# Four groups of scale columns in place of five in the K projection of a DiT block

## The chip, the cores and the metric

The kernel runs on one core of one Trainium2 chip. The metric is the device time of one execution in microseconds (us); the number for a kernel is the median of its runs. A core has five engines with queues of their own: TensorE (PE; its weight loads are listed as PEld), VectorE (DVE), ScalarE (ACT), GpSimd (POOL) and SyncE (SP), which here issues nearly all of the transfers from memory. Engines wait for each other, and for transfers, by semaphores.

## The reference

One block of a diffusion transformer on two batches of 256 tokens, width D = 1152, two heads:

```python
B, N, D = (2, 256, 1152)          # F = 4 * D
mod = (_silu(c) @ w_mod).reshape(B, 6, 1, D)
shift_a, scale_a, gate_a, shift_m, scale_m, gate_m = [mod[:, i] for i in range(6)]
h = _layernorm(x, axis=-1) * (1 + scale_a) + shift_a
qkv = (h @ wqkv).reshape(B, N, 3, H, Dh)
...
x = x + gate_a * a
h2 = _layernorm(x, axis=-1) * (1 + scale_m) + shift_m
m = _gelu(h2 @ w_fc1) @ w_fc2
return x + gate_m * m
```

The part that matters here is `h`, without its shift, and the K third of `h @ wqkv`.

## The kernel before

The 512 tokens are four tiles of 128 (tiles 0 and 1 are batch 0, tiles 2 and 3 batch 1). The width of 1152 is nine chunks of 128. The kernel runs through its stages in one written order; at its end a loop (L813 to L823) ties every instruction to the one before it on its engine, so each engine's order is that of the program text.

**Loads.** SP issues, in this order, the four tiles of x (L86) and then, by the list `SGROUPS` (L98), for each group of chunks the columns of the scale part of `w_mod` that belong to it (`w_scale_a`, L107) and the rows of `w_k` that belong to it, without their last three column blocks (`load_k`, L104). The first group's rows go as two transfers, one for each row, the others' as one. Then come the last three column blocks of all rows of `w_k` (L113), the shift columns (L129), `w_q` (L134) and the rest. A load of columns a-b of the scale moves 128 partitions x 9 rows x (b - a + 1) x 128 values of two bytes, so a group of one, two or three chunks is made of pieces of 256, 512 or 768 bytes.

**Front.** ScalarE and VectorE make the layer norm's statistics; `norm1` writes the normalized tokens `xn`; TensorE transposes them chunk by chunk (`transpose_x`, L264) into PSUM tiles `pt`. The factor 1 + scale_a of a chunk comes from `scale_group` (L241): nine products of 128x128 weights with two columns for each chunk, written to a PSUM tile `pm`; `scale_add` (L253) adds 1 to it on VectorE and stores it in `scale_a`. `pm` and `pt` share two PSUM buffers in turn ("aux"). `both` (L317) then scales a transposed chunk into `hT0`: batch 0 on VectorE (L270), after it batch 1 on ScalarE (L272). A chunk is then ready for `k_step(k)`, whose matmuls (L280) add chunk k's part of the K projection to six PSUM tiles, `pk[0]` to `pk[5]`.

**The loop around the change** (L396 to L404) does this for steps k = 3 to 8:

```python
    for k in range(3, KD):
        split = 2 if k == 5 else 0
        k_step(k, 0, T, 0, split)
        if k in (3, 5, 7):
            k1 = min(k + 3, KD)
            scale_add(scale_group(k + 1, k1), k + 1, k1)
        if k < KD - 1:
            both(transpose_x([k + 1], range(NT)), k + 1)
        k_step(k, 0, T, split)
```

So ahead of step 3's six matmuls come the scale products of chunks 4-5 (18 of them) and chunk 4's four transposes; ahead of step 4's, chunk 5's transposes; inside step 5, after two of its matmuls, the products of chunks 6-7 and chunk 6's transposes; ahead of step 6's, chunk 7's transposes; ahead of step 7's, the products of chunk 8 and its transposes. Chunks 0 to 3 are served by the code above the loop (L360 to L395), which the diff leaves alone. After the loop, `k_evac` (L405) empties the six tiles and `k_panel` (L437) computes the last three column blocks of K. The Q projection (L521), attention (L556, L639), V (L599), the output projection (L690) and the MLP (L743, L799) follow.

Of the kernel before, what the change touches and what calls it, by code (L numbers as in the profile page):

```python
# [19 lines left out]
def kernel(  # L20
# [20 lines left out]
    KD = D // P  # L41
# [18 lines left out]
    def acc_tile(shape, name, dt=FP32):  # L60
        return psum.tile(shape, dt, name=name, tag="acc", bufs=6)
# [33 lines left out]
    sT = act.tile([P, KD, SW], BF16, name="sT")  # L95
    nc.gpsimd.memset(sT[:], 0.0)

    SGROUPS = [(0, 2), (2, 4), (4, 6), (6, 8), (8, 9)]  # L98
    KM1 = 6
    w_scale_a = wide_tile("w_scale_a")  # L100
    w_k = wide_tile("w_k")
# [1 line left out]
    def load_k(k0, k1, c0, c1):  # L103
        nc.sync.dma_start(w_k[:, k0:k1, c0:c1], wqkv_v[:, k0:k1, D + c0:D + c1])  # L104

    for k0, k1 in SGROUPS:
        nc.sync.dma_start(  # L107
            w_scale_a[:, :, k0 * P:k1 * P],
            wmod_v[:, :, S_SCALE_A * D + k0 * P:S_SCALE_A * D + k1 * P],
        )  # L110
        for a, z in [(0, 1), (1, 2)] if k0 == 0 else [(k0, k1)]:
            load_k(a, z, 0, KM1 * P)
    load_k(0, KD, KM1 * P, D)  # L113

# [126 lines left out]
    def scale_group(k0, k1, tile_of=aux_tile):  # L241
        pm = tile_of([P, k1 - k0, B], "pm")
        for j in range(k0, k1):
            if j == 0:
                nc.tensor.matmul(pm[:, 0, :], ones_row[:], ones_row[:, 0:B], start=True, stop=False)
            for k in range(KD):
                nc.tensor.matmul(  # L247
                    pm[:, j - k0, :], w_scale_a[:, k, j * P:(j + 1) * P], sT[:, k, 0:B],
                    start=(k == 0 and j > 0), stop=(k == KD - 1),
                )  # L250
        return pm

    def scale_add(pm, k0, k1, eng="d"):  # L253
        if eng == "a":
            nc.scalar.activation(scale_a[:, k0:k1, :], pm[:], ACT.Identity, bias=ones[:])
        else:
            nc.vector.tensor_scalar_add(scale_a[:, k0:k1, :], pm[:], 1.0)

    def transpose_x(ks, ts, pt=None, j0=0):
        if pt is None:  # L260
            pt = aux_tile([P, len(ks), len(ts) * P], "pt", BF16)
        for j, t in enumerate(ts, j0):
            for i, k in enumerate(ks):
                nc.tensor.transpose(pt[:, i, j * P:(j + 1) * P], xns[t][:, k * P:(k + 1) * P], ident[:])  # L264
        return pt
# [10 lines left out]
    def k_step(k, c0=0, c1=T, m0=0, m1=KM1):  # L276
        for m in range(m0, m1):
            if k == 0 and c0 == 0:
                pk[m] = acc_tile([P, T], "pk")
            nc.tensor.matmul(  # L280
                pk[m][:, c0:c1], w_k[:, k, m * P:(m + 1) * P], hT0[:, k, c0:c1],
                start=(k == 0 and c0 == 0), stop=(k == KD - 1), skip_group_check=True,
            )
# [33 lines left out]
    def both(pt, k):  # L317
        for b, e in enumerate("da"):
            modulate(pt, 0, k, b, b * N, e)
# [73 lines left out]
    norm1(3, CUT, D)  # L393
    k_step(2, 0, N)
    k_step(2, N, T)  # L395
    for k in range(3, KD):  # L396
        split = 2 if k == 5 else 0
        k_step(k, 0, T, 0, split)
        if k in (3, 5, 7):
            k1 = min(k + 3, KD)  # L400
            scale_add(scale_group(k + 1, k1), k + 1, k1)
        if k < KD - 1:
            both(transpose_x([k + 1], range(NT)), k + 1)
        k_step(k, 0, T, split)  # L404
# [449 lines left out]
```

## Time and profile before

| | |
|---|---|
| median of 3 runs (243.22 to 243.6) | 243.32 us |
| the profiled execution: its time, its span | 243.6 us, 241.8 us |
| TensorE, VectorE, ScalarE busy | 235.4, 91.5, 59.9 us |
| granted TensorE clock, mean | 0.998 |
| moved by transfers | 53.29 MB |
| K matmuls of the steps (L280), 128x512 or 128x256 | 13.1 us busy in 70 records |
| loads of scale columns, L107, issue to landing (shortest, middle, longest of five) | 6.6, 7.2, 7.4 us |

The span runs from the first to the last instruction of one profiled execution; about 1.8 us of its time lie around it. A matmul's record holds the time to its end, which overlaps with the next one's; the spacing of starts, or the chain of waits, tells what one costs in a row of them. Some matmul records are missing (72 were issued on L280). An idle time is listed with what ended it, its releaser. In the order of time, neighbouring instructions of one line are merged into one row: start, time from the first's start to the last's end, engine, line, operation, the tiles written and read, shape, count.

### The profile page before, as it was taken

The page shows a single profiled execution, that of the slowest core. Times are in us where ns is not written, and L with a number is a line of the kernel's source. Part 1 is how long each engine was busy: PE and PEld are TensorE (multiplying, and loading weights), DVE is VectorE, ACT ScalarE, POOL GpSimd, SP SyncE. Part 2 cuts the span into 40 slices and gives each one's busy share as a digit, 9 for nine tenths or more (in the row PEclk, how much of TensorE's full clock was granted, in tenths as well). Part 3 has the DMA queues.
Part 4 walks back from the last instruction along what each step waited for, and adds up shares of the span by engine and source line. Part 5 has one row for each costly group of instructions (what it writes and reads, how often), then busy time and mean ns, then how long its engine had stood idle before and what let it go on. Part 6 is the DMA issues. An engine that isn't in the chain of part 4 may idle for free.

```text
span 241.8 us, 3979 instructions
## 1 busy us (share of the span) xinstructions
PE 235.4 (97%) x1688; PEld 144.4 (60%) x1698; DVE 91.5 (38%) x193; ACT 59.9 (25%) x121; POOL 28.3 (12%) x47
## 2 busy tenths in 40 slices
PE   8799999999999999999999999999999999999994
PEld 5585444465567566888844444444556665566674
DVE  3742442319325678830002999960010000000001
ACT  6633322307215032671422333222000000000000
POOL 2300000002300324100000000001121111111111
PEclk9999999999999999999999999999999999999999
DMA  6999999997579999239999999999200000000000
GB/s 188 327 317 310 378 366 393 389 391 247 147 263 398 387 377 159 49 59 361 391 391 391 340 327 284 274 327 284 98 16 16 20 16 16 19 18 19 27 23 16
DMA packets 48781, 53.29 MB, mean 220 GB/s; under 512 B 9587, under 2 KB 36475, under 8 KB 48763
## 3 DMA queue, kind: packets, MB, share of 16 engines
q1 hardware_dynamic: 41312, 50.14, 62.5%
q10 hardware_dynamic: 6939, 1.71, 4.7%
q0 software_dynamic: 512, 1.19, 1.5%
q8 instruction: 13, 0.21, 0.4%
q14 instruction: 5, 0.04, 0.0%
HBM read 50.14 MB, written 1.19 MB: 212 GB/s over the span
## 4 chain that ended last, share of the span: by engine, by line
PE 94%; issue 2%; ACT 2%; POOL 1%; DVE 0%; POOLq 0%; DVEq 0%; ACTq 0%
PE pacc L799 29%; PE pacc L743 29%; PE pacc L690 7%; PE pacc L599 7%; PE pq L521 7%; PE pk L280 5%; PE pk L309 2%; PE pa L639 2%; PE ps_s L556 2%; PE pn L416 2%; ACT sink L206 1%; PE pt L264 1%; PE pm L247 1%; PE pg L498 0%; ACT rstd L335 0%
## 5 line engine op out<-in xcount | busy, mean ns | idle before, releaser
L743 PE MATMUL pacc<-hT,w_f 128*128 128x256 bf16 (+1 forms) x427 | 70.3, 325 | 0.3
L799 PE MATMUL pacc<-w_f,gT 128*128 128x384 bf16 (+2 forms) x468 | 70.5, 314 | 0.0
L799 PEld LDWEIGHTS <-gT 128*128 128x128 bf16 x468 | 44.4, 98 | 26.2
L743 PEld LDWEIGHTS <-w_f 128*128 128x128 bf16 x432 | 42.2, 98 | 27.6
L805 DVE TENSOR_TENSOR tmp<-pacc,gate 128x384 f32<-128x384 f32 (+2 forms) x13 | 6.9, 527 | 65.6 <-PE pacc L799 57.2
L775 ACT ACTIVATE gT<-pacc 128x512 bf16<-128x512 f32 x24 | 14.3, 597 | 32.6 <-PE pacc L743 32.6
L469 DVE SCALAR_TENSOR_TENSOR part<-w_gate_m,s,part 128x1152 f32<-128x1152 bf16 x16 | 21.4, 1414 | 0.0
L807 POOL TENSOR_TENSOR o_sb<-tmp,x 128x384 bf16<-128x384 f32 (+1 forms) x12 | 11.7, 973 | 54.0 <-DVE tmp L805 54.0
L690 PE MATMUL pacc<-w_o,big 128*128 128x384 bf16 x108 | 17.9, 326 | 0.0
L521 PE MATMUL pq<-hT,w_q 128*128 128x512 bf16 x79 | 17.7, 379 | 0.1
L599 PE MATMUL pacc<-w_v,hT 128*128 128x384 bf16 x108 | 17.7, 326 | 0.0
L599 PEld LDWEIGHTS <-hT 128*128 128x128 bf16 x108 | 10.5, 98 | 7.1 <-issue 0.3
L690 PEld LDWEIGHTS <-big 128*128 128x128 bf16 x108 | 10.4, 98 | 7.2 <-issue 0.4
L521 PEld LDWEIGHTS <-w_q 128*128 128x128 bf16 x81 | 7.9, 98 | 9.4
L280 PE MATMUL pk<-big,w_k 128*128 128x256 bf16 (+1 forms) x70 | 13.1, 324 | 0.1
L696 POOL TENSOR_TENSOR x<-tmp,x_sb 128x384 f32<-128x384 f32 x8 | 7.3, 914 | 27.4 <-DVE tmp L695 27.4
L467 DVE TENSOR_SCALAR part<-w_gate_m,s 128x1152 f32<-128x1152 bf16 x2 | 1.6, 818 | 22.3 <-DMA w_gate_m<-in_w_mod_dram 22.3
L491 POOL DMA_DIRECT2D gates_dram<-nat_v x2 | 1.1, 536 | 67.7 <-DVE nat_v L489 67.7
L280 PEld LDWEIGHTS <-w_k 128*128 128x128 bf16 x72 | 6.7, 97 | 3.7 <-issue 0.3
L764 ACT ACTIVATE gT<-pacc 128x512 bf16<-128x512 f32 x12 | 6.5, 598 | 8.9 <-PE pacc L743 8.9
L512 POOL DMA_DIRECT2D gates_dram<-nat x4 | 2.3, 584 | 49.3 <-DVE nat L509 48.7
L695 DVE TENSOR_TENSOR tmp<-pacc,gate 128x384 f32<-128x384 f32 x12 | 6.6, 549 | 3.1 <-PE pacc L690 3.1
(102 smaller groups left out, 164.2 us busy)
## 6 DMA issues: line engine op xcount, KB each, us to landing
w_f<-in_w_fc_dram SPq DMA_DIRECT2D x12, 864.0 KB, 14.9
w_f<-in_w_fc_dram SPq DMA_DIRECT2D x3, 1728.0 KB, 7.9
w_f<-in_w_fc_dram SPq DMA_DIRECT2D x2, 2592.0 KB, 17.2
w_gate_a<-in_w_mod_dram SPq DMA_DIRECT2D x3, 864.0 KB, 11.9
w_v<-in_wqkv_dram SPq DMA_DIRECT2D x3, 864.0 KB, 13.8
w_o<-in_wo_dram SPq DMA_DIRECT2D x3, 864.0 KB, 14.0
w_shift_m<-in_w_mod_dram SPq DMA_DIRECT2D x3, 864.0 KB, 6.6
w_scale_m<-in_w_mod_dram SPq DMA_DIRECT2D x3, 864.0 KB, 12.1
```

The lines of the kernel that those rows point to most:

```text
L280: nc.tensor.matmul(pk[m][:, c0:c1], w_k[:, k, m * P:(m + 1) * P], hT0[:, k, c0:c1], start=(k == 0 and c0 == 0), stop=(k == KD - 1), skip_g ...
L469: nc.vector.scalar_tensor_tensor(part[:, b, :], wg[:, k, :], s32[:, k, b:b + 1], part[:, b, :], op0=ALU.mult, op1=ALU.add,)
L521: nc.tensor.matmul(pq[m][:], w_q[:, k, m * P:(m + 1) * P], hT[:, k, :], start=(k == 0), stop=(k == KD - 1), skip_group_check=True,)
L599: nc.tensor.matmul(pacc[:], hT[:, k, t * P:(t + 1) * P], w_v[:, k, pnl * PW:(pnl + 1) * PW], start=(k == 0), stop=(k == KD - 1),)
L690: nc.tensor.matmul(pacc[:], aT[:, k, t * P:(t + 1) * P], w_o[:, k, c0:c1], start=(k == 0), stop=(k == KD - 1),)
L695: nc.vector.tensor_tensor(tmp[:], pacc[:], gate_a[:, b, c0:c1], op=ALU.mult)
L696: (nc.gpsimd if pool_add else nc.vector).tensor_tensor(x1[:, t, c0:c1], tmp[:], x_sb[:, t, c0:c1], op=ALU.add)
L743: nc.tensor.matmul(dst, w_f1[m // KD][:, k, ml * P:(ml + 1) * P], hT[:, k, c0:c1], start=start, stop=(k == KD - 1), **kw,)
L775: nc.scalar.activation(gT[:, m, :], pacc[:], ACT.Gelu_apprx_tanh)
L799: nc.tensor.matmul(pacc[:], gT[:, kk, t * P:(t + 1) * P], w_f2[j][:, r, c0 - n * PW:c0 - n * PW + cw], start=(kk == 0), stop=(kk == KF - 1),)
L805: nc.vector.tensor_tensor(tmp[:], pacc[:], gate_m[:, b, c0:c0 + cw], op=ALU.mult)
L807: (nc.vector if last else nc.gpsimd).tensor_tensor(o_sb[:], tmp[:], x1[:, t, c0:c0 + cw], op=ALU.add)
```

## The change

The scale columns come in four groups, chunks 0-1, 2-3, 4-6 and 7-8, where they came in five (0-1, 2-3, 4-5, 6-7, 8). The rows of `w_k` for chunks 4-6 come as two transfers, row 4 and rows 5-6; rows 7-8 as one. Of the products of chunks 4-6, chunk 4's nine stand inside step 3, after two of its six matmuls, and those of chunks 5-6 inside step 4, likewise; those of chunks 7-8 stand inside step 6. After them, still inside the step, come the transposes and scalings of the next chunk, then the step's other four matmuls. Steps 5, 7 and 8 are not split; in steps 5 and 7 the next chunk's transposes stand ahead of the six matmuls.

```diff
-    SGROUPS = [(0, 2), (2, 4), (4, 6), (6, 8), (8, 9)]
+    SGROUPS = [(0, 2), (2, 4), (4, 7), (7, 9)]
...
-        for a, z in [(0, 1), (1, 2)] if k0 == 0 else [(k0, k1)]:
+        ends = {0: (1, 2), 4: (5, 7)}.get(k0, (k1,))
+        for a, z in zip((k0,) + ends, ends):
             load_k(a, z, 0, KM1 * P)
...
     k_step(2, N, T)
+    INSIDE = {3: (2, (4, 5)), 4: (2, (5, 7)), 6: (2, (7, 9))}
     for k in range(3, KD):
-        split = 2 if k == 5 else 0
+        split, group = INSIDE.get(k, (0, None))
         k_step(k, 0, T, 0, split)
-        if k in (3, 5, 7):
-            k1 = min(k + 3, KD)
-            scale_add(scale_group(k + 1, k1), k + 1, k1)
+        if group:
+            scale_add(scale_group(*group), *group)
         if k < KD - 1:
             both(transpose_x([k + 1], range(NT)), k + 1)
         k_step(k, 0, T, split)
```

## The prediction, made before the changed kernel was run

> **What bounds the kernel now.** I read the chain of waits first, then its part from 15 to 27 us, then the order of time in that stretch, and last the loads.
>
> From the page: the busy shares, and the chain that ended last.
>
> ```profile
> PE 235.4 (97%) x1688; PEld 144.4 (60%) x1698; DVE 91.5 (38%) x193; ACT 59.9 (25%) x121; POOL 28.3 (12%) x47
> PE 94%; issue 2%; ACT 2%; POOL 1%; DVE 0%; POOLq 0%; DVEq 0%; ACTq 0%
> ```
>
> TensorE is the chain for 94% of the span, so an edit is worth what it adds to or takes from TensorE's time, unless it acts in the first 11 us, where the statistics decide. The changed steps run between 15 and 26 us. Their chain:
>
> ```profile
> 15.82 0.43 PE pm L247 x18
> 16.25 0.24 PE pt L264 x4
> ...
> 18.01 1.73 PE pk L280 x8
> 19.74 0.43 PE pm L247 x18
> 20.16 0.24 PE pt L264 x4
> 20.41 0.86 PE pk L280 x4
> 21.27 0.22 PE pt L264 x4
> ...
> 22.84 0.20 PE pm L247 x9
> 23.04 0.24 PE pt L264 x4
> 23.29 2.59 PE pk L280 x12
> ```
>
> One piece begins where the last ended: scale products, transposes and K matmuls stand back to back. Prices: a 512-wide K matmul 0.216 us (2.59 by 12), a scale product 0.024 (0.43 by 18), a set of four transposes 0.22. Two rows of the order of time show the only place with no slack:
>
> ```profile
> 20.03 0.38 PE L264 MATMUL pt<-ident,xn 128*128 128x128 bf16 x4
> 20.86 0.47 ACT L272 ACTIVATE big<-pt,scale_a 128x256 bf16<-128x256 bf16 x1 [1.95 <-DVE big L270]
> 21.39 1.45 PE L280 MATMUL pk<-big,w_k 128*128 128x512 bf16 x5
> ```
>
> Chunk 6's transposes start at 20.03; VectorE scales batch 0, ScalarE follows it with batch 1 and ends at 20.86 + 0.47 = 21.33; step 6's first matmul starts at 21.39. So **from the start of a chunk's transposes to the first matmul on it is at least 1.36 us**, of which TensorE must fill the rest. In this place it fills four transposes (0.22), four matmuls (0.86) and chunk 7's transposes (0.22), 1.30 in all: it already stands 0.05 us.
>
> The loads:
>
> ```profile
> w_scale_a<-in_w_mod_dram SPq DMA_DIRECT2D x1, 576.0 KB, 7.4
> w_k<-in_wqkv_dram SPq DMA_DIRECT2D x1, 384.0 KB, 8.1
> ```
>
> These are the transfers issued at 7.86 (scale columns 4-5) and 5.19 us (w_k rows 2-3, just ahead in the queue). They land at 7.86 + 7.4 = 15.3 and 5.19 + 8.1 = 13.3, so 576 KB of 512-byte pieces took 2.0 us of the queue. The weight loads of chunks 4-5's scale products begin at 15.55 (order of time), 0.25 after the landing.
>
> **The change, part by part.**
>
> *Work.* TensorE's instructions are the same in number and form, as are the eight pairs of modulations; four scale additions stay four up to a size of 128x4 (0.16 us, beside TensorE). SP issues one transfer fewer (0.47 us of a queue that TensorE isn't shown waiting for). Sum: 0.
>
> *Order.* Chunk k+1's transposes are followed by fewer matmuls of step k. I lay TensorE's rows out again, each chunk's first use against the 1.36 us:
> - Chunk 4 (transposed inside step 3): then come four matmuls of step 3, 0.86, and at once step 4's first two, since step 4 is now split too, with no transposes between. Cover 0.22 + 0.86 = 1.08; TensorE stands 1.36 - 1.08 = **0.28 us**. Before, six matmuls and chunk 5's transposes stood there (1.73), no wait.
> - Chunk 5 (inside step 4): four matmuls and chunk 6's transposes, 1.30; wait **0.05**. Before: 0.22 + 1.30 = 1.52, no wait.
> - Chunk 6 (ahead of an unsplit step 5): 0.22 + 1.30 = 1.52; none, in place of 0.05: **-0.05**.
> - Chunk 7 (inside step 6): as chunk 6 before, **0.05**. Chunk 8: six matmuls, 1.52, none.
> - Chunk 3 at the front: its ScalarE half ends at 14.93 + 0.47 = 15.40 and step 3 now starts at 15.65, when step 2 is done; none.
>
> Queued behind the waiting matmul are, on TensorE, everything else; nobody else is late, since VectorE and ScalarE idle there. The stall is not absorbed later: no row of TensorE's waits after 26 us names another engine or a transfer. Sum of the order: 0.28 + 0.05 - 0.05 + 0.05 = **+0.33 us**. From below, the three positive terms could lose 0.05 each to rounding of starts, so +0.18; from above, if the 0.16 us scale addition ahead of VectorE's scaling came to lie wholly in the path at each of three split places, +0.8, but the 1.36 us was read at a place that has it already, so I take 0.33.
>
> *Loads.* Scale columns 4-6 come as one transfer of 864 KB (884,736 bytes) in 768-byte pieces where 576 KB stood; TensorE needs them not at 15.55 but two matmuls later, 15.55 + 0.43 = 15.98. What 768-byte pieces cost is shown by the rest of w_k, the same 864 KB form; the stretches of time (us, then each engine's busy time, clock, share and GB/s of the transfers):
>
> ```profile
> 13.00:13.50 0.50, 0.50 (x21) 0.50 (x18) 0.08 (x1) 0.00 (x0) 0.00 (x0) 1.00 1.21 294
> 21.00:22.30 1.30, 1.25 (x10) 0.70 (x9) 0.35 (x1) 0.71 (x2) 0.00 (x0) 1.00 1.11 333
> ```
>
> At 333 GB/s the transfer takes 2.66 us and lands at 13.3 + 2.66 = 15.96, 0.02 us before it is needed; at the 294 GB/s of the 512-byte pieces 3.0 us, 16.3, and TensorE waits 0.33. Bounds 0 and 0.33; I take 0.02, by the row of the same piece size and a pickup of some 0.02-0.04 (x_sb's statistics on VectorE start that soon after a landing). The Trainium skill speaks of this too: "DMA: Bandwidth & Descriptors", section Specifications, gives about 358 GB/s as a core's limit from HBM. By it the load would be in after an estimated 2.47 us with 0.2 us to spare, and the sum would be the order's alone; the page of this profile has slices of 393 GB/s, above that limit, and small pieces below it, so the row of the piece size is used. The later loads have room: w_k row 4 (192 KB) lands some 0.6 us after, at 16.6, for a step that starts at 17.7; columns 7-8 by about 19.7 for products at 21.6; w_k rows 7-8 by 21 for a step at 23.4. All told the queue moves the same bytes with fewer short pieces and runs some 0.6 us ahead afterwards, which nothing on TensorE's path collects.
>
> **Sum.** 0.33 + 0.02 = +0.35 us: span 241.8 to 242.15. The profiled execution took 243.6 with its span of 241.8 (1.8 around it) and was the slowest of three; against the median of 243.32 the sum gives **243.67 us**, +0.14%. From here, 0.2% (0.49 us) is about what a measurement of this kernel can tell from no change.
>
> **The rivals.**
> - *The load is late* (slower). Place: the weight loads of chunk 4's product, with everything on TensorE behind them. For: 0.02 us of room in one execution, in a queue whose landings from issue range from 7.2 to 7.4 us for like loads. Against: the same-form row. Price: with 294 GB/s, 0.33 + 0.33 = +0.66, 243.98 us. It carries the change over 0.2% once the landing is 0.16 us behind need, at 16.14.
> - *The stall is longer than read* (slower): the scale addition adds its 0.16 us at the places where the split is new, steps 3 and 4, if VectorE starts later against the transposes than at 20.03. +0.35 + 0.32 = 243.99 us. Against: the same sequence stands at 22.9 to 24.2 us with nine products and keeps the same distance.
> - *The stall doesn't show, and the room gains* (faster): if the 1.36 us were TensorE's own order and not a wait for ScalarE, the changed order would drop the 0.05 and give 243.27. For a gain beyond 0.49 us TensorE would need idle time to remove, and the chain has 0.05 in this stretch; only an earlier start of the first 11 us, which the diff doesn't touch, could do it: 242.8.
>
> **How the numbers follow.** Forecast as worked out (stall of 0.3, load in time) 0.58; load late 0.22; longer stall 0.13; no stall or a gain 0.07 (0.02 of it within the bound). The forecast lies 0.14 us under the bound of 0.49, so a part of its share (about 0.06) ends above it by scatter alone; the two slower rivals lie above. Faster 0.05, within 0.54, slower 0.41. Range: the likeliest's own is 243.5 to 243.85; taking in the rivals' 243.98, some scatter of the medians (243.22 to 243.6 among three runs of one kernel) and a little of the no-stall case gives 243.25 to 244.15.
>
> **What will show it.** In the changed profile: step 4's first matmul starting some 0.05 us after ScalarE's scaling of chunk 4 ends, with about 0.28 us of nothing before it; 0.05 us ahead of steps 5 and 7 and none ahead of step 6; the last K matmul of step 8 near 0.35 us later than before, and the same shift at the end of the span. The load is judged by the first scale product of chunk 4: a start at about 16.1 means in time, later means the first rival. The prediction is wrong if step 4 starts without a gap, if the shift at 26 us isn't the shift at the end, or if a later stage waits for a transfer.

## The result, and the profile after

The changed kernel took **244.78 us** (median of 4 runs, 244.36 to 244.88), beside 243.33 us for the kernel before on the same chip (4 runs, 243.22 to 243.6). The ratio is 1.0055, with a 95% interval of 1.0037 to 1.0072: slower by about 0.6%. The forecast was 243.67 us, and the time lies above the whole range of 243.25 to 244.15.

The profiled execution took 244.79 us with a span of 243.0, 1.2 us more than the 241.8 before. Two lines of the changed kernel's page: the chain that ended last by engine, and the group of the MLP's first matmuls (busy time, mean ns of one, then idle time ahead of it and what ended that). Line numbers are one higher than before.

```profile
PE 88%; DMA 5%; SPq 3%; DVE 1%; ACT 1%; issue 1%; DVEq 0%; ACTq 0%
L744 PE MATMUL pacc<-hT,w_f 128*128 128x256 bf16 (+1 forms) x427 | 70.3, 325 | 0.8 <-DVE hT L663 0.6
```

TensorE was the chain for 94% of the span; now it is 88%, and transfers and SP's queue have 8% of it. The last row is a place that the prediction didn't look at: the MLP's first matmul, 73 us behind the edited loop, waits for VectorE's `hT`.

The chain of waits of the changed kernel between 5 and 30 us (start, length, what), where the edited loop runs:

```profile
8.00 8.13 DMA w_scale_a<-in_w_mod_dram
16.13 0.05 issue
16.17 0.38 PE pm L248 x9
16.55 0.26 PE pt L265 x4
...
17.24 0.48 ACT big L273
17.73 0.04 issue
17.77 0.59 PE pk L281 x2
```

And in the order of time, a set of four transposes with the matmuls behind it: of the kernel before where nothing waits, then of the changed kernel at step 5:

```profile
17.62 0.39 PE L264 MATMUL pt<-ident,xn 128*128 128x128 bf16 x4
17.85 1.89 PE L280 MATMUL pk<-big,w_k 128*128 128x512 bf16 x8
```

```profile
19.73 0.39 PE L265 MATMUL pt<-ident,xn 128*128 128x128 bf16 x4
20.01 1.89 PE L281 MATMUL pk<-big,w_k 128*128 128x512 bf16 x7
```

Three things stand where TensorE's pieces stood end to end. Chunk 4's products start at 16.17, when the load of columns 4-6, issued at 8.00, has landed: a wait of 0.25 us, since the two matmuls ahead of them (from 15.49 on, 0.216 us each) were through at 15.93. Step 4's first matmul starts at 17.77, when ScalarE has scaled chunk 4 (17.24 + 0.48 = 17.72); the matmul ahead of it started at 17.28, so TensorE stood 17.77 - 17.28 - 0.216 = 0.27 us. And step 5's first matmul starts 0.28 us after the transposes ahead of it, where 0.23 is the distance without a wait: 0.05 us, and the same in step 7. (Pieces of 0.05 us called "issue" elsewhere in a chain, behind a K matmul and ahead of the next PE piece, are places where one matmul's record is missing: the starts on their two sides are one matmul of 0.216 us further apart than they would otherwise be.) From the end of step 2 to the first matmul of the panel the changed kernel takes 10.63 us and the one before 10.06: **0.57 us are lost in the edited loop**.

The chain of waits between 70 and 100 us, first of the changed kernel, then of the one before:

```profile
89.31 1.58 PE pacc L691 x9
...
93.12 0.93 ACT xn L681
94.05 0.02 issue
94.07 4.21 DMA hT<-xn
...
98.38 0.36 DVE hT L663
```

```profile
86.58 2.32 PE pn L416 x72
88.90 8.88 PE pacc L690 x54
97.78 2.29 PE pacc L743 x21
```

Before, the output projection's matmuls (L690) run into the MLP's (L743) without a break. After, the projection ends at 98.03 and the MLP starts at 98.78. The chain goes by way of the second transpose of the normalized tokens, a transfer issued at 94.07 (ACT's queue, `hT<-xn`), which took 4.21 us to land. **Another 0.75 us are lost here.** The span's account: 0.16 us of an earlier front (step 2 ended at 15.49 in place of 15.65, above the edited loop), 0.57 in the loop, 0.75 ahead of the MLP, 0.06 at the very end: -0.16 + 0.57 + 0.75 + 0.06 = 1.22.

The transfers that matter, in the view by tile (issues: shortest/middle/longest ns, first and last start in us; or issue to landing in us). Of the kernel before: the normalized tokens' transposes from issue to landing, the softmax transposes, the gate's broadcast and the first load after attention, each from its tile's answer (the broadcast's row has the two transfers for `gate_a` here and two for the MLP's gate at 171 us):

```profile
DMA to landing us min/median/max: 3.2/3.2/8.4
...
L550 ACTq DMA_TRANSPOSE soft<-soft x4: 1212/1228/1267, 57.8 to 62.6; - x4
...
L456 POOL DMA_DIRECT2D gate<-gates_dram x4: 558/565/586, 63.3 to 171.7; - x4
...
L120 SPq DMA_DIRECT2D w_shift_m<-in_w_mod_dram x3: 367/487/488, 67.1 to 68.0; - x3
```

The same of the changed kernel:

```profile
DMA to landing us min/median/max: 3.2/4.2/9.6
...
L551 ACTq DMA_TRANSPOSE soft<-soft x4: 1204/1218/1263, 58.3 to 63.0; - x4
...
L457 POOL DMA_DIRECT2D gate<-gates_dram x4: 558/565/586, 63.7 to 173.5; - x4
...
L121 SPq DMA_DIRECT2D w_shift_m<-in_w_mod_dram x3: 368/488/488, 68.2 to 69.1; - x3
```

The program ties the first load after attention (`w_shift_m`, L615) to the landing of the last softmax transpose, the fourth. From the issue of that transpose it was 67.06 - 62.64 = 4.42 us before and 68.19 - 63.04 = 5.15 after. Behind it stand 8.8 MB of loads. In the packets' records those end 0.94 us after the issue of the second token transpose before, and 2.67 us after it in the changed kernel; and that transpose, which runs beside them, moves its last data 2.74 and 3.72 us after its issue.

So two questions: why was the load of columns 4-6 late, and why did a change at 15 to 26 us push the loads at 67 to 97 us onto a transpose?

### The profile page after: what moved, and what is told of

It reads as the page before. It is cut to its first block, busy times and chain, and to the rows that moved or that the text cites. A ratio compares the mean times of both kernels' runs of the same rounds, so it can differ in the third digit from the quotient of the medians.

```text
span 243.0 us, 3978 instructions
## 1 busy us (share of the span) xinstructions
PE 236.7 (97%) x1687; PEld 145.1 (60%) x1698; DVE 91.5 (38%) x193; ACT 60.2 (25%) x121; POOL 28.3 (12%) x47
## 4 chain that ended last, share of the span: by engine, by line
PE 88%; DMA 5%; SPq 3%; DVE 1%; ACT 1%; issue 1%; DVEq 0%; ACTq 0%
PE pacc L800 29%; PE pacc L744 29%; PE pacc L600 7%; PE pq L522 7%; PE pacc L691 4%; DMA w_scale_a<-in_w_mod_dram 3%; PE pk L281 3%; PE pk L310 2%; SPq L104 2%; DMA hT<-xn 2%; PE pa L640 2%; PE ps_s L557 2%; PE pn L417 2%; SPq L86 1%; PE pm L248 1%
## 5 line engine op out<-in xcount | busy, mean ns | idle before, releaser
L174 PE MATMUL pwarm<-zeros 128*128 128x256 f32 x18 | 7.4, 586 | 1.2 <-DVE eps_t L93 1.2
```

What stands on the lines that cost most here:

```text
L174: nc.tensor.matmul(dst[:, 0:T // 2], zeros32[:, 0:P], zeros32, start=True, stop=True)
```

## Experiments: which part costs what

*The old load groups with the new order of work, and the new groups with the old order.*

```diff
-    SGROUPS = [(0, 2), (2, 4), (4, 7), (7, 9)]
+    SGROUPS = [(0, 2), (2, 4), (4, 6), (6, 8), (8, 9)]
```

> The new order of products and splits with the five old load groups. In the changed kernel TensorE lost time in three places: 0.25 us ahead of chunk 4's products (load late), 0.27 us ahead of step 4 (no cover), and 0.75 us at the start of the MLP, at 98 us, where it waits for a transposed tile. By the order theory this kernel keeps the step-4 wait (0.27) and the 0.05 ahead of steps 5 and 7, and has no wait ahead of chunk 4's products, for columns 4-5 land at about 15.3; it may wait up to 0.15 us in chunk 6's product for columns 6-7 (landing at about 18.3): about +0.4 to 0.45 us at 26 us. If the loss at 98 us follows from any such delay (theory D), the end is about +1.1 us or more, near 244.5; if it belongs to the new loads (theory L), the end is the local loss alone, near 243.8.

> The four new load groups with the old order. Local: columns 4-6 land at about 16.0 to 16.1 where the old order needs them at 15.55, so TensorE waits about 0.45 to 0.55 us there; 0.05 ahead of step 6 as before, and no step-4 wait: about +0.45 to 0.5 at 26 us. Theory D (any delay brings the loss at 98 us): about 244.5 at the end. Theory L (the new loads bring it): also near 244.5. If neither, 243.8.

The new order with the old loads: ratio 1.0103 (1.0066 to 1.0139). This ratio can't be used as it stands: five of its seven runs show a granted clock of 0.993 and take some 247 us, while two, the profiled one among them, have 1.0 and take 244.46 and 244.68 us. The trace is clear: step 4 waits 0.27 us as in the changed kernel, and the products of chunks 5-6 wait 0.37 us in their middle, since column 6 came with the group of columns 6-7 and that is still under way; 10.76 us for the loop, and 0.36 us ahead of the MLP. The same kernel again on another chip (below) took 244.32 us in one run.

The new loads with the old order: 1.0055 (1.0036 to 1.0073), as slow as the whole change. The old order wants columns 4-5 at once and then columns 6-7 together, and the bigger groups bring both late: 0.57 us ahead of the products of chunks 4-5 and 1.00 us inside those of 6-7, a loop of 11.66 us. Ahead of the MLP its profile has 0.10 us. The chain of this kernel between 14 and 27 us:

```profile
11.26 9.62 DMA w_scale_a<-in_w_mod_dram
20.88 0.05 issue
20.93 0.38 PE pm L248 x9
```

Neither half alone was as fast as the kernel before in these runs. The step-4 wait belongs to the order, the wait ahead of chunk 4's products to the groups. The second loss goes with neither half: the old loads had 0.36 us of it in that profile, the new ones 0.10.

*Is a delay in the K stage by itself enough to bring the second loss?* The kernel before, with the 18 products of chunks 4-5 done twice (the first set is started over by the second), which puts 0.43 us more on TensorE at the same place.

```diff
-            for k in range(KD):
+            for k in (list(range(KD)) if j in again else []) + list(range(KD)):
...
-            scale_add(scale_group(k + 1, k1), k + 1, k1)
+            scale_add(scale_group(k + 1, k1, again=(4, 5)), k + 1, k1)
```

> The kernel before, with the 18 products of chunks 4-5 made twice: a pure delay of TensorE of 18 x 0.024 = 0.43 us at 16 us, old loads and old order. Theory D: the delay alone brings a wait at the start of the MLP, and the end is later by more than the delay, about +1.1 us, 244.4 or more. Theory L: the delay passes to the end as it is, +0.43, 243.75, and no wait at 98 us.

Ratio 1.0003 (0.999 to 1.0017); in the profile the loop takes 10.62 us, 0.55 more than before (the added products, and 0.09 ahead of the first of them for their load), almost the changed kernel's 10.63. But nothing follows from it:

```profile
89.35 8.88 PE pacc L690 x54
98.23 1.86 PE pacc L743 x17
```

The projection runs into the MLP as before, and the first load comes 4.41 us after the last softmax transpose. So the second loss isn't the first one's shadow: as much delay, with the old loads and the old order, didn't bring it in this execution. The span, 242.2, is 0.4 longer than in the first profile of the kernel before, as the prediction's rule says (what is added to TensorE arrives at the end). The ratio doesn't show it: 0.43 us would be 1.0018, just above its interval.

*Let the loads after attention go earlier.* The wait of these loads is tied to the third softmax transpose in place of the fourth; once with the changed kernel and once with the kernel before.

```diff
-            transposed = softmaxes[i]()
+            made = softmaxes[i]()
+            transposed = made if i < 3 else transposed
```

> The changed kernel with one edit: the loads after attention (w_shift_m first) wait for the third attention transpose and not for the fourth, whose landing in the changed kernel took 5.1 us from issue beside the gate's broadcast (4.4 before). If the wait of 0.75 us at 98 us comes from the loads starting late and so running into the layer-norm transposes (theory: late loads), it goes, and the end is at about 243.33 + 0.55 = 243.9, or less. If the 98 us wait has another cause, the end stays near 244.8. If the fourth transpose, now beside the loads, comes too late for the attention product at 74 us, a new wait appears there.

> The kernel before, its loads after attention released by the third attention transpose. Theory of the late loads: no stall at the MLP's start in any execution, so the median is at or below that of before (0 to -0.5 us) and the scatter of its runs is smaller; against the same edit in the changed kernel (+0.33 on its chip) it shows the local loss alone, 0.4 to 0.6 us. If the stall never touches before, no change.

The changed kernel with this edit: 1.0006 (0.9995 to 1.0017) to the kernel before, where the changed kernel itself in the next group of runs had 1.0035. Its chain keeps both waits of the loop (0.35 us for the load in this execution, 0.27 ahead of step 4) and has lost the one ahead of the MLP, as the projection runs on into it:

```profile
89.14 8.88 PE pacc L692 x54
98.02 2.07 PE pacc L745 x19
```

The kernel before gains nothing by it: 0.9995 (0.9986 to 1.0004). That is what a cause in the loads after attention asks for: where they end in time, an earlier start is worth nothing; where they don't, it takes the second loss away.

*Take the gate's broadcast out of the way.* GpSimd issues the broadcast of `gate_a` to 128 partitions 0.6 us after the last softmax transpose (63.04 and 63.7 us in the lines above). In the packets' records of the changed kernel that transpose's data are through 1.84 us after its issue; the few bytes with which it tells SP that it has landed come among the broadcast's 4.6 KB packets, the last of them at 4.77 us. Here the broadcast is done in the seventh of the V projection's twelve groups in place of the first.

```diff
-        if i == 0:
+        if i == 6:
             gate_a = gate_finish()
```

> The changed kernel beside the kernel before on this chip. So far the stall at the MLP's start goes with the time from the issue of the fourth attention transpose to the first load after it: 4.4 us and no stall (before, the delayed kernel), 5.15 us and 0.75 us (the changed kernel). Theory S (the stall is the changed kernel's own): about 1.0055 of before again, with a wait of some 0.7 us ahead of the MLP. Theory R (it is drawn anew in each execution, and the kernel before has it at times): a ratio nearer to 1.0025 (local loss 0.57 us), with or without the wait in this trace.

> The changed kernel with the gate's copies, writes and broadcast moved behind the V groups 0 to 5, after the attention transposes. If the broadcast's packets hold up the fourth transpose (theory: broadcast ahead of it on the transfer engines), that transpose lands 2.5 us from issue like the three others, the loads start about 2.5 us earlier, and the 0.75 us at the MLP's start are gone: the local loss remains, +0.4 to 0.6 us on before. If the transpose still takes 4.4 to 5.1 us, the broadcast isn't its cause.

The changed kernel once more on this chip: 1.0035 (1.002 to 1.0051), and in its profile 0.38 us ahead of the MLP. With the late broadcast: 1.0015 (1.0004 to 1.0026). SP's queue in the order of time, of the second kernel:

```profile
65.37 1.43 SPq L121 DMA_DIRECT2D w_shift_m<-in_w_mod_dram  x3
```

The last softmax transpose was issued at 62.91, so the first load follows it by 2.46 us (4.89 in the changed kernel here), and the MLP starts without a wait. **So the second loss goes by this path: broadcast, landing of the last softmax transpose, loads after attention, second token transpose, MLP.** What is left is the loop: in this execution 0.46 us for the load and 0.27 ahead of step 4.

*The step-4 wait.* In the changed kernel step 4 isn't split, so chunks 5-6's products stand ahead of it and cover ScalarE's work.

```diff
-    INSIDE = {3: (2, (4, 5)), 4: (2, (5, 7)), 6: (2, (7, 9))}
+    INSIDE = {3: (2, (4, 5)), 4: (0, (5, 7)), 6: (2, (7, 9))}
```

> The changed kernel with step 4 whole: the products of chunks 5-6 and chunk 5's transposes ahead of its six matmuls. Chunk 4's scaling then has 0.86 + 0.43 + 0.22 + 0.22 us of cover for the 1.36: the 0.27 us ahead of step 4 go, the wait of 0.25 us for the columns of chunks 4-6 and 0.05 ahead of step 7 stay (chunk 5 then has 1.52, no wait). From the end of step 2 to the first panel 0.3 us less than in the changed kernel (10.63): about 10.3. At the end 0.3 us less, if the wait at the MLP's start is the same.

The 0.27 is gone; the load wait is 0.32 and the loop takes 10.39. Ratio 1.0027 (1.0014 to 1.0039); the MLP still waited 0.69 us in the profile.

*The load wait.* In the changed kernel chunk 4's columns get a group of their own, so there are five loads again, 4 and 5-6 in place of 4-6.

```diff
-    SGROUPS = [(0, 2), (2, 4), (4, 7), (7, 9)]
+    SGROUPS = [(0, 2), (2, 4), (4, 5), (5, 7), (7, 9)]
```

> The changed kernel with chunk 4's scale columns as a load of their own (288 KB), then chunks 5-6 and 7-8: five loads, the new order of products. Chunk 4's columns land near 14.7, before they are needed (15.5 + 0.43): the wait ahead of its products, 0.25 to 0.7 us in the traces of the changed loads, goes; the 0.27 us ahead of step 4 and 0.05 ahead of steps 5 and 7 stay. From the end of step 2 to the first panel 10.06 + 0.33 = 10.4 us. At the end less than the changed kernel by the wait that is gone, if the stall at the MLP's start is alike.

Ratio 0.9999 (0.9983 to 1.0015). The chain between 14 and 27 us:

```profile
14.74 1.74 PE pk L281 x14
16.48 0.20 PE pm L248 x9
...
17.38 0.48 ACT big L273
17.86 0.04 issue
17.90 0.59 PE pk L281 x2
```

Chunk 4's products follow the matmuls at once; the step-4 wait stays (0.27), the loop takes 10.37 us, 0.31 more than before: the prediction's order term. Ahead of the MLP 0.10 us are left. So in the trace the new order costs 0.3 us, and the load wait is gone with the bigger group; the ratio can neither show nor exclude so little.

*A try at a faster kernel that missed.* The kernel before, split after one matmul in steps 3 and 5 and with the late broadcast.

> The kernel before with its five loads and three edits: steps 3 and 5 split after one matmul (the products of 4-5 one matmul later, those of 6-7 one matmul earlier) and the gate's copies and broadcast behind the V groups 0 to 5. Each chunk then has 1.52 us of cover for the 1.36, so no wait for a scaling; the columns of 4-5 are needed 0.22 us later than before; no stall at the MLP's start. From the end of step 2 to the first panel 10.0 us; the median 0.1 to 0.3 us under before on this chip.

0.9997 (0.9983 to 1.0011): no gain. It has lost the 0.05 us of the kernel before, but the products of chunks 6-7, now a matmul earlier, wait 0.61 us for their load.

*A repeat of the kernel before, and more load in front of attention.* In the second, the last third of `w_o` is loaded twice, to see whether a transfer queue that is busy for longer ahead of the last softmax transpose changes the broadcast's pace.

```diff
     w_o = load_rows("w_o", wo_v, 0)
+    nc.sync.dma_start(w_o[:, 6:9, :], wo_v[:, 6:9, :])
```

> A second trace of the kernel before. If the broadcast's pace is drawn anew in each execution (theory R), its fourth attention transpose may take anything from 4.4 to 5.2 us, with a stall at the MLP's start where it is over about 4.6. If the pace belongs to the kernel (theory S), it takes 4.4 again and there is no stall.

> The changed kernel with one load more after w_o: its last third, loaded a second time (864 KB, the same values). The queue of loads then ends some 2 us later, as late against the attention transposes as in the kernel before or later. If the broadcast is slow in the changed kernel because memory had been idle for about 1 us longer ahead of it, the fourth transpose takes about 4.4 us now and the stall at the MLP's start is under 0.1 us. If not, it takes 4.7 to 5.3 as in the other traces with the new loads. The local loss at 26 us is unchanged, 0.5 to 0.6.

The repeat took 243.44 us in one run, without a wait ahead of the MLP (4.37 us from transpose to first load), but with 0.19 us ahead of the products of chunks 4-5, because its front was 0.33 us earlier than in the first profile and the load wasn't: the kernel before stands at the edge of its loads, too (0.19 us there as well in the profile of its variant with the earlier loads after attention). In the groups of runs behind the first its medians are 243.64 to 243.95 us in place of 243.33, and no run shows why; so a ratio near 1 there doesn't say that a kernel lost nothing, and the waits in the traces decide. The reload lost 0.68 us ahead of the MLP (244.98 us in one run), but by another path, since the broadcast moved behind the added load and met the loads after attention; it doesn't answer the question.

## Experiments: the pace of the transfers

In the packets' records the broadcast's first 32 packets take 213 and 230 ns (medians of two profiles) in the kernel before and 400 and 464 in the changed one. One idea was the number of transfers that SP issues ahead of it: 39 before, 38 in the changed kernel.

> The changed kernel with one small transfer more (4 KB of x into an unused tile, behind the loads of w_k), so that SP issues 39 transfers again. Theory N (the number of transfers turns the order of the semaphores and with it the broadcast's pace): the fourth attention transpose lands 4.4 to 4.5 us from issue, the stall at the MLP's start is 0 to 0.1 us, and the median is 0.4 to 0.6 us over before, the local loss. Theory G (it goes with the four groups) or chance: 4.8 to 5.3 us, stall 0.3 to 0.75, about 1 us over before.

> The kernel before with the last two loads of w_q (two rows each) as one, so that SP issues 38 transfers; K stage untouched. Theory N: the fourth attention transpose takes 4.8 us or more and a stall of 0.3 us or more stands at the MLP's start; the median is 0.3 to 0.7 us over before. Theory G: 4.4, no stall, same time.

> The same with the first two loads of w_q merged too, 37 transfers. Theory N: off the 4.4 us as well, or back to it if only odd counts matter. Theory G: 4.4 us, no stall.

> A second trace of the new order with the five old load groups (39 transfers), whose first trace had 4.73 us and a stall of 0.36 us at the MLP's start. Theory N: 4.4 to 4.5 as for the other kernels with 39 transfers, the first one being chance. If it is 4.7 again, the number of transfers isn't all.

The first of the four is the changed kernel with a 39th transfer of 4 KB into a spare tile:

```diff
     load_k(0, KD, KM1 * P, D)
+    spare = const.tile([P, 16], BF16, name="spare")
+    nc.sync.dma_start(spare[:], x_v[:, 0, 0, 0:16])
```

It took 243.57 us, ratio 0.9991 (0.9979 to 1.0004): no load wait, no wait ahead of the MLP. The kernel before with two of the four `w_q` loads merged (38 transfers) took 243.8, 1.0005 (0.9989 to 1.0021), with 0.16 us ahead of the MLP; with the other two merged as well (37) 245.01 us in one run, with 0.65 us there, but also 0.94 us ahead of the Q projection for the merged load, so that its number shows little. The repeat of the new order with the old loads (39) had no wait ahead of the MLP, 244.32 us in one run; its first profile had 0.36. The count fits most of these traces, but the trace with the 39th transfer showed something else: from 12 to 14 us its loads already moved 361 GB/s, in place of 338 in the changed kernel, and the added transfer was issued only at 15.08 us.

What differs from the start is the address. The spare tile takes 32 bytes of every partition, and all buffers that lie behind it are 32 bytes further on: in the built programs `w_scale_a` moves from byte 101088 of its partition to 101120 and `w_k` from 184032 to 184064, from 224 beyond a multiple of 256 to a multiple of 256. Rows of 2304 bytes and pieces of 256, 512 and 768 keep them there. So two kernels got the shift without a transfer or any other instruction, by a wider tile ahead of the others:

```diff
-    eps_t = const.tile([P, 1], FP32, name="eps_t")
-    nc.vector.memset(eps_t[:], LN_EPS)
+    eps_w = const.tile([P, 9], FP32, name="eps_w")
+    eps_t = eps_w[:, 0:1]
+    nc.vector.memset(eps_t, LN_EPS)
```

> The kernel before, with the tile of the LayerNorm epsilon 36 bytes wide per partition in place of 4, of which one column is used as before; no instruction is added or changed, but every buffer allocated after it, those of all weight loads among them, begins 32 bytes further in its partition (at a multiple of 64 bytes in place of 32 beyond one). Theory A (the alignment of the load's target sets the pace): 576 KB scale loads take about 1.72 us in place of 2.0 to 2.1, the slices of the page move up to 410 GB/s, the wide loads before attention end some 4 us earlier, the wait of 0.05 us or less ahead of a product group stays nothing, and, since no wait of the kernel before hung on a load, the time is that of the kernel before within 0.2%: 243.2 to 243.8 us. Theory N (the extra transfer of the run before it made the difference): paces and times as in the kernel before, 1.99 to 2.1 us per scale load.

> The changed kernel with the same 32 bytes of shift and no other edit, so still with 38 transfers on the SyncE queue. Theory A (alignment): columns 4-6 land at about 15.4 us of the span in place of 16.13, the wait of 0.25 us ahead of chunk 4's products is gone and the 0.27 us ahead of step 4 stays; the loads after attention don't meet the second LN2 transpose, so no wait ahead of the MLP; in all 0.25 + 0.75 = about 1.0 us less than the changed kernel where that showed 244.8, 243.4 to 243.9 us, and a ratio to the kernel before of 0.999 to 1.0015. Theory N (the 39th transfer did it): the wait ahead of chunk 4's products stays at 0.25 us or more and the MLP's first product waits 0.4 to 0.75 us, 244.4 to 244.9 us, ratio 1.003 to 1.0055.

| | us, median (runs) | ratio to the kernel before | loop, us | wait for columns 4-6 | ahead of the MLP |
|---|---|---|---|---|---|
| before | 243.33 (4) | | 10.06 | | 0 |
| changed | 244.78 (4) | 1.0055 (1.0037 to 1.0072) | 10.63 | 0.25 | 0.75 |
| before, shifted | 243.21 (12) | 0.9968 (0.9949 to 0.9988) | 10.06 | | 0 |
| changed, shifted | 243.64 (12) | 0.9998 (0.9983 to 1.0012) | 10.38 | 0 | 0 |

The two shifted kernels shared their chip with the kernel before at 243.7 us (243.14 to 245.69, 23 runs). Stretches of 2 us (length, busy time of the five engines, clock, share, GB/s), before and before shifted:

```profile
12.00:14.00 2.00, 2.00 (x35) 1.74 (x33) 1.27 (x6) 0.47 (x1) 0.00 (x0) 1.00 1.17 313
```

```profile
12.00:14.00 2.00, 2.00 (x39) 1.89 (x37) 1.27 (x5) 0.52 (x2) 0.00 (x0) 1.00 1.11 368
```

And the scale columns' five loads from issue to landing in the shifted kernel, beside 6.6, 7.2 and 7.4 us before:

```profile
DMA to landing us min/median/max: 6.1/6.2/6.6
```

From the packets' records, a 512-byte piece takes 31.2 ns before and 27.4 shifted, one of 768 bytes 40.7 and 36.0 (the two changed kernels), 1536 bytes 78.3 and 66.5, 2304 bytes 101.2 and 95.3 (means over the loads of the front). The edit adds no instruction and no transfer and moves every later buffer alike, so the addresses do it; that it is the load's own target, and not another buffer that moved with it, is the nearest reading, not a separate test. The chain of the changed kernel, shifted, between 5 and 30 us:

```profile
14.06 1.53 PE pk L282 x13
15.59 0.05 issue
15.64 0.37 PE pm L249 x9
16.01 0.26 PE pt L266 x4
...
16.70 0.48 ACT big L274
17.18 0.04 issue
17.22 0.59 PE pk L282 x2
```

The products follow the matmuls without a wait (a matmul's record is missing ahead of the 0.05 us) and no load is in the chain; the step-4 wait is the same 0.27 us. The loop takes 10.38 in place of 10.06, 0.32 more. The first load after attention still comes late, 5.08 us after the last softmax transpose, but the faster loads end 1.38 us after the second token transpose's issue in place of 2.67, and the MLP doesn't wait. With both kernels shifted, on one chip and in the same group of runs, the change costs 243.64 - 243.21 = 0.43 us, near its order term of 0.32. The kernel before, shifted, beats both kernels of this study. Its profile is the kernel before's with a front 0.36 us earlier, like the repeat's above, and no wait behind it; its expectation of "within 0.2%" was a little too small a gain. What it gains shows in its runs: ten of twelve lie between 243.11 and 243.3 us, while 21 of the 23 of the kernel before on this chip were above 243.3.

## Why the prediction was wrong

**The order of the work was right.** Predicted for the step-4 wait 0.28 us, measured 0.27 in every trace that has this order; 0.05 at steps 5 and 7, measured 0.05; 0.33 in all, and 0.32 measured as soon as the loads are out of the way (shifted kernels), 0.31 with columns 4 on their own. The minimum of 1.36 us from a chunk's transposes to its first matmul, read from one row of the kernel before, held.

**The load term was mis-sized: 0.02 predicted, 0.25 measured**, and 0.11 to 0.46 in the other profiles of kernels with the same loads and the split of step 3. The duration taken for the transfer was nearly right: the load took 2.70 us in place of 2.66. Two small things were not: the load ahead of it landed 0.13 us later than taken (13.43 in place of 13.3); and the products' turn came at 15.93 in place of 15.98, since this execution's front was 0.16 us earlier (the forecast counted from the weight loads, 0.1 ahead of the matmuls) and the predicted 15.98 was tied to the old front. The 0.04 us between landing and start had been allowed for: 0.02 + 0.04 + 0.13 + 0.05 is the 0.25 measured, within rounding. (The landings of like loads, given as 7.2 to 7.4 us from issue, leave out the first group's 6.6.) The rival "the load is late" had the right place, and the 16.13 of the landing is where it said that it would decide. The mistake was to take a slack of 0.02 us, read from one execution, for a term near nothing: the end of step 2 lies between 15.19 and 15.89 us in the traces of this study, and a load doesn't follow the front. Near zero slack such scatter only costs, and the waits of 0.11 to 0.46 are that cost. The Trainium skill's rule that the prediction set aside ("DMA: Bandwidth & Descriptors", section Specifications: about 358 GB/s from HBM for a core) lies between the 313 and 338 GB/s of the kernels before and changed from 12 to 14 us and the 413 GB/s of the best slice of the kernel before, shifted; it decides neither.

**"The stall is not absorbed later: no row of TensorE's waits after 26 us names another engine or a transfer" was the step that failed: in its place the MLP waited another 0.75 us for a transpose that met running loads.** The sentence says what waits in the kernel before, not how near to waiting a later stage stands. The second token transpose overlapped the last loads by 0.94 us already and the MLP started without a wait; with 1.64 to 2.12 us of overlap other traces wait 0 to 0.38 us, and with 2.5 to 2.7 us 0.64 to 0.75. So the room was about a microsecond, and the trace of before shows its parts: a transpose of 3.2 us, issued while loads still ran, whose result the MLP's first matmul needs. The prediction named it as what would make it wrong ("if a later stage waits for a transfer"), but gave it no price and no share. The other sentence on what comes later, that the queue runs "some 0.6 us ahead afterwards, which nothing on TensorE's path collects", had its size right (the loads ahead of attention end at 58.50 us in place of 59.15); whether that lead has a part in the second loss, no run shows. With the two terms put right the sum is 0.33 + 0.25 + 0.75 = 1.33 us for the profiled execution (1.22 in its span, whose front was 0.16 earlier); in the changed kernel's second profile it is 0.32 + 0.11 + 0.38 = 0.81, and its span of 242.5 is 0.7 longer than before.

**What stays open.** Why the first load after attention comes 4.4 us after the last softmax transpose in most traces of the kernel before and 4.9 to 5.3 in those of the changed one. It hangs on the pace of the broadcast's packets and on when the broadcast is issued: where GpSimd issued it 1.0 us after the transpose in place of 0.6 (the kernel before shifted, and the run with the spare transfer), the load followed at 2.53 us. Neither the delay in the loop (4.41) nor the shift (5.08 in the changed kernel) decides it; the count of transfers fits most traces, but the new order with the old loads (4.73 and 4.40 with the same program) shows that a part is scatter. So the path of the second loss is shown, and why the change sets it off isn't.

## What to carry to other kernels

A transfer that lands within a few tenths of a microsecond of its need isn't a term of nothing: price it by the spread of fronts and landings, not by the one execution that is profiled. When an early change touches the transfers, look through the later stages for those that meet running loads with little room (here a transpose issued into the tail of a prefetch), and give each a price, although no row of waits names them yet. And look where the buffers begin: 32 bytes took as much off the changed kernel's ratio (1.0035 to 1.0055 down to 0.9998, against the kernel before as it was) as its schedule had cost.

## What the runs showed of the chip that was not expected

- **Moving the buffers changes the loads' pace.** With targets at multiples of 256 bytes in place of 224 beyond one, the same loads ran at 368 in place of 313 GB/s from 12 to 14 us, and pieces of 512 bytes took 27.4 in place of 31.2 ns. The Trainium skill has a rule that points there ("DMA: Bandwidth & Descriptors", section How a descriptor splits into AXI transactions): a descriptor that doesn't start at a multiple of 256 bytes also fetches what lies between the boundary below it and its start, and pays beats for it. The page tells this of what is read. Put on the side that is written, and counted as in its table, 512 bytes from 224 on need 23 beats in place of 16, an estimate of 1.44 times. The runs agree in direction, not in size: 31.2 / 27.4 = 1.14 for 512 bytes, 1.18 for 1536 (78.3 / 66.5), 1.06 for 2304. Whether a multiple of 64 would do was not tried.
- **A landing is told late while another queue's packets are under way**: 4.4 to 5.3 us from the issue of a softmax transpose to the load that waits for it with the broadcast behind it, 2.5 without. The transpose's data are through 1.84 and 1.85 us after its issue in the changed kernel and with the late broadcast; its last few bytes follow at 4.77 and at 2.04 us.
